# Two decode layers on one core: the feed-forward in one part of 448 columns, loads of 3.5 and 14 KB, and eight tiles of the last w2 in 512-column products

## The chip, the cores and the metric

The kernel runs on one core of a Trainium2 chip. The time is that of the whole kernel on the device, in microseconds; the median of 3 runs before the change is 705.18 us (705.13 to 705.38). Names of engines are those of the profile: PE is TensorE (PEld its weight loads), DVE VectorE, ACT ScalarE, POOL GpSimd, SP the SyncE whose queue issues nearly all loads.

## The reference

Four tokens (B = 4, one position each, D = 512) go twice through an attention block with a cache and a gated feed-forward; both layers use the same weights and the same cache. All is float32.

```python
def _A_ref(x, k_cache, v_cache, wq, wo):   # Hq 32, Hkv 8, Sk 4096, Dh 128
    q = (x @ wq).reshape(B, Sq, Hq, Dh).transpose(0, 2, 1, 3)
    k, v = jnp.repeat(k_cache, 4, axis=1), jnp.repeat(v_cache, 4, axis=1)
    p = _softmax(jnp.einsum("bhqd,bhkd->bhqk", q, k) * Dh ** -0.5)
    return jnp.einsum("bhqk,bhkd->bhqd", p, v).transpose(0, 2, 1, 3).reshape(B, Sq, Hq * Dh) @ wo
def _B_ref(x, w1, w3, w2):                 # F = 1792
    return (_silu(x @ w1) * (x @ w3)) @ w2
for layer in range(2):
    x = x + _A_ref(_layernorm(x), k_cache, v_cache, wq, wo)
    x = x + _B_ref(_layernorm(x), w1, w3, w2)
```

## The kernel before

Nearly all of the time is reading: keys, values and weights, for two layers, about 298 MB. One large SBUF tile, `arena` (218 pieces of 1 KB in each of the 128 partitions), receives every load. `plan` is the list of all loads in order; `pump` issues as many of them on the SP queue as find room, and `done` and `vacate` give room back (and call `pump`) when the products that read a load have been recorded. So a load is issued once the PE instruction that last read its place is through; the list order is fixed. Eight semaphores serve the loads in turn, so a load also waits for the landing of the eighth load before it. Around the first layer's feed-forward the places are given out by hand (`slots`, seven places of 4 KB in a row, and `RING`); elsewhere the first free stretch is taken.

The chain of a layer is: attention over 8 key/value groups, `project_o` (times wo, summed in `x_ps`), `collect` (residual and mean), then `feed_forward`, and after the first layer `collect` again and the next layer's queries. The order of the instructions on each engine is that of the code (manual schedule). `busy(n)` puts n products of 128 columns on PE whose result nobody reads (L292).

The 1792 columns of w1 and w3 are cut into four blocks of 448 (`FJ`), one for each 32-row group of PSUM; so a product of one 128-row chunk of x with all columns is four matmuls that write to `s_ps` (w1) or `o_ps` (w3). Before the change each block is again in two parts: the first 256 columns (`FA`) and the last 192 (`FB`). In `feed_forward` part a of w1 and w3 is done first (L561, L566), `gate` and `join` (L530, L535) make its h = silu(w1 x) (w3 x), then part b of w1 (L573), the transposes of h's first 256 columns (L577) and `tiles`, part b of w3, `join` of the last 192 columns (L593) and the transposes of those (`tail_tiles`, L595). In layer 0 (`keep`), `down` multiplies pairs of w2 tiles, its first call stands between the products of w3's part b (L591), and products with `busy` stand after most chunks. In layer 1 the output is made with swapped roles (`columns`, L550: the four 128-column blocks of a w2 tile go to four row groups of `x_ps`, so that the result comes out 128 columns wide). The 8 tiles of 16 rows in `few` (L555; w2's first tile cut up, loaded as `w2s` by `aside`) are multiplied in two halves, L588 and L608; the 13 other tiles follow in L610 to L614. At last `y` (L664) is copied from `x_ps` and stored.

The loads of layer 0 are 512 KB (a parts, w2) and 384 KB (b parts) each; in layer 1 w1 and w3 come in two loads each, 16 KB and 12 KB per partition, and tiles 1 to 13 of w2 in loads of 4, 4, 2, 2 and 1 tiles.

Of the kernel before, what the change touches and what calls it, by code (L numbers as in the profile page):

```python
# [9 lines left out]
AF = mybir.ActivationFunctionType  # L10
# [10 lines left out]
NI = BK // P  # L21
GW = SK * B
FJ = F // 4
FA = 2 * P
FB = FJ - FA
WT = 14
FEW = 16
EPS = 1e-5
SCALE = DH ** -0.5
# [9 lines left out]
def tile_decode_layers(ctx: ExitStack, tc: tile.TileContext, x, kt, v, wq, wo, w1, w3, w2, w2s, out):  # L39
# [48 lines left out]
    def load(src, per, keys, at=None):  # L88
        plan.append((src, per, keys, at))
# [9 lines left out]
    def weights(name, src, layer, parts, per, at=None, first=0):  # L99
        r = 0  # L100
        for n in parts:
            load(src[:, r * KB:(r + n) * KB], per, [(name, layer, first + r // per + j) for j in range(n // per)],
                 None if at is None else at + r)
            r += n

# [10 lines left out]

    def piece(name, i, at):

        w, layer, lo, n, per = {"w1a": (w1, 0, 4 * i, 4, 4), "w3a": (w3, 0, 4 * i, 4, 4),
                                "w1b": (w1, 0, 16 + 3 * i, 3, 3), "w3b": (w3, 0, 16 + 3 * i, 3, 3),  # L120
                                "w2": (w2, 0, 4 * i, 4, 2), "half": (kt[TURN], 1, 4 * i, 4, 4)}[name]
        weights(name, w[:, lo * KB:(lo + n) * KB], layer, (n,), per, at, 2 * i if name == "w2" else i)

    RING = KEPT + 64
    slots = [WO] + [RING + 4 * i for i in (5, 4, 3, 2, 1, 0)]
    for i in range(4):
        piece("w1a", i, (slots[6], slots[1], slots[2], slots[3])[i])
    for i in range(4):
        piece("w3a", i, (slots[4], slots[5], slots[0], slots[6])[i])
    for i in range(4):  # L130
        piece("w1b", i, RING + 21 - 3 * i)
    for i in range(2):
        piece("w3b", i, RING + 9 - 3 * i)
    piece("w2", 0, slots[0])
    for i in range(2, 4):
        piece("w3b", i, RING + 9 - 3 * i)
    for i in range(1, 7):
        piece("w2", i, slots[i])
# [25 lines left out]
    def pump():  # L164
        while state["next"] < len(plan):
            src, per, keys, at = plan[state["next"]]
            n = src.shape[-1] // KB
# [12 lines left out]
            if a is None:  # L180
                return
            nc.sync.dma_start(arena[:, a * KB:(a + n) * KB], src)  # L182
            i = state["next"]
            if i == 0:
                nc.sync.dma_start(xt[:8], x[:8])
            left[i] = (len(keys), a, n)
            for j, key in enumerate(keys):
                where[key] = (a + j * per, per, i)
            state["next"] += 1

    def loaded(*key):
        a, n, _ = where[key]
        return arena[:, a * KB:(a + n) * KB]
# [102 lines left out]
    def chunk(k):  # L296
        return p[:, k * P:(k + 1) * P]
# [219 lines left out]
    def feed_forward(layer, mean):  # L517
        keep = layer < LAYERS - 1
        h = p[:, 0:FJ]

        def product(name, ps, lo, n, fill=(0, 0, 0, 0), ks=range(KC)):
            for k in ks:
                w = loaded(name, layer, k)
                for j in range(4):
                    nc.tensor.matmul(ps[32 * j:32 * j + 32, lo:lo + n], x32[:, k, :], w[:, j * n:(j + 1) * n],  # L525
                                     start=(k == 0), stop=(k == KC - 1))
                done(name, layer, k)
                busy(fill[k] if keep else 0)

        def gate(lo, n):  # L530
            a = h[:, lo:lo + n]
            nc.scalar.activation(a, s_ps[:, lo:lo + n], AF.Sigmoid, scale=rstd)
            nc.vector.scalar_tensor_tensor(a, s_ps[:, lo:lo + n], rstd, a, op0=ALU.mult, op1=ALU.mult)

        def join(lo, n):  # L535
            a = h[:, lo:lo + n]
            nc.vector.scalar_tensor_tensor(a, o_ps[:, lo:lo + n], rstd, a, op0=ALU.mult, op1=ALU.mult)
# [12 lines left out]
        def columns(rows, m, w, last=False):  # L550
            for k in range(KC):
                nc.tensor.matmul(x_ps[32 * k:32 * k + B, 0:P], hT[rows, m, :], w[rows, k * P:(k + 1) * P],  # L552
                                 start=False, stop=last)
# [7 lines left out]
        product("w1a", s_ps, 0, FA, (0, 0, 2, 0))  # L561
# [4 lines left out]
        product("w3a", o_ps, 0, FA, (2, 2, 2, 2))  # L566
        if not keep:
            for k in range(KC):
                nc.tensor.matmul(x_ps[32 * k:32 * k + B, 0:P], xt[:, k, :], ident, start=True, stop=False)
            busy(4)  # L570
        gate(0, FA)
        join(0, FA)
        product("w1b", s_ps, FA, FB, (1, 1, 1, 1))  # L573
        if keep:
            gate(FA, FB)
            nc.scalar.activation(spare, half, AF.Exp)
        for i in range(2):  # L577
            nc.tensor.transpose(t_ps[:, i, :], h[:, i * P:(i + 1) * P], ident)
        if not keep:
            for u in range(8):  # L580
                nc.tensor.matmul(t_ps[0:FEW, 2, B * u:B * u + B], h[0:32, FEW * u:FEW * u + FEW], ident[0:32, 0:B],
                                 start=True, stop=True)
            busy()
        tiles(0, 8)
        if not keep:
            nc.vector.tensor_copy(hT[0:FEW, WT:WT + 8, :], t_ps[0:FEW, 2, 0:8 * B].rearrange("p (u b) -> p u b", b=B))
            gate(FA, FB)
            few(0, 4)  # L588
        product("w3b", o_ps, FA, FB, (1, 2, 1, 1), range(0, 2))
        if keep:  # L590
            down(0)  # L591
        product("w3b", o_ps, FA, FB, (1, 2, 1, 1), range(2, KC))
        join(FA, FB)  # L593

        def tail_tiles():  # L595
            nc.tensor.transpose(t_ps[:, 2, :], h[:, FA:FA + P], ident)
            for u in (0, 64):
                nc.tensor.matmul(t_ps[u:u + 64, 3, 0:64], h[u:u + 64, FA + P:FJ], ident[u:u + 64, u:u + 64],
                                 start=True, stop=True)
            tiles(8, 6)  # L600

        if keep:
            for i in range(1, WT // 2):
                if i == 4:
                    tail_tiles()
                down(i)
            return
        few(4, 8)  # L608
        tail_tiles()
        for m in range(1, WT):  # L610
# [96 lines left out]
```

## Time and profile before

| | |
|---|---|
| median of 3 runs | 705.18 us (705.13 to 705.38) |
| span of the profiled execution, first to last instruction | 705.4 us |
| its time around the span | not listed; the span alone is 0.2 us above the median |
| PE, PEld, DVE, ACT busy | 405.0, 136.0, 85.2, 38.0 us |
| DMA over the span | 298.85 MB, mean 424 GB/s |
| mean granted PE clock | 0.814 of full speed |

The profile is one execution. Its page gives busy times by engine, the span in 40 slices, the queues of the DMA engines, the chain of work that ended last, and groups of instructions. Views of the trace give the same for a stretch of time: the timeline (start, duration, engine, line, operation, tiles and shapes, count, and in brackets the engine's idle time before it and what ended it), the windows (busy time of each engine, granted clock and DMA share of each stretch), the waits, and the DMA queues. A matmul of float32 counts as two instructions in the profile, and one in the program's order below.

### The profile page before, as it was taken

The numbers are of one execution on the slowest core, as the hardware profiler recorded it, in microseconds if no ns is written. First come the engines' busy times: TensorE is split into PE (matmuls) and PEld (weight loads), VectorE is DVE, ScalarE is ACT, GpSimd is POOL, SyncE is SP. The second block draws the span as 40 slices with busy tenths as digits, with TensorE's granted clock in tenths as the row PEclk, the third lists the DMA queues.
The fourth block names the chain that finished last, engine by engine and source line by source line (L and its number), as shares of the span: only waits on it lengthen the run. The fifth ranks groups of instructions, "written<-read, shape, count | busy, mean of one in ns | idle before, by whom it ended". The sixth has DMA issues, their size and how long they took to land. (4 is left out here: it accounts for less than half of the span.)

```text
span 705.4 us, 7077 instructions
## 1 busy us (share of the span) xinstructions
PE 405.0 (57%) x3172; PEld 136.0 (19%) x3172; DVE 85.2 (12%) x291; ACT 38.0 (5%) x87; POOL 3.5 (0%) x11
## 2 busy tenths in 40 slices
PE   2555453555565453547788884365564545367686
PEld 1112111111111111112243321011111111112244
DVE  2001010101001010101111111020000101010120
ACT  0000000000000000002001000000000000000100
POOL 0000000000000000000000000000000000000000
PEclk9976687767778777779999997588787878787899
DMA  9999999999999999999999999999999999999996
GB/s 417 428 406 461 425 420 421 461 417 431 439 431 432 427 443 420 442 417 429 409 403 406 394 438 447 431 427 439 436 427 435 432 439 425 431 423 430 424 423 261
DMA packets 13605, 298.85 MB, mean 424 GB/s; under 512 B 1655, under 2 KB 1783, under 8 KB 6263
## 3 DMA queue, kind: packets, MB, share of 16 engines
q1 hardware_dynamic: 13440, 298.39, 99.0%
q8 instruction: 25, 0.41, 0.2%
q14 instruction: 5, 0.04, 0.0%
q10 hardware_dynamic: 135, 0.01, 0.0%
HBM read 298.33 MB, written 0.07 MB: 423 GB/s over the span
## 5 line engine op out<-in xcount | busy, mean ns | idle before, releaser
L457 PE MATMUL o_ps<-arena 128*32 128x512 f32 x1024 | 143.3, 707 | 148.1 <-DMA arena<-in_v 135.2
L410 PE MATMUL s_ps<-arena,qpad 128*32 128x512 f32 x1020 | 148.1, 734 | 90.3 <-DMA arena<-in_kt 90.3
L457 PEld LDWEIGHTS o_ps<-arena 128*32 128x32 f32 x1024 | 36.9, 127 | 251.9 <-issue 221.1
L410 PEld LDWEIGHTS s_ps<-arena,qpad 128*32 128x32 f32 x1020 | 39.3, 132 | 182.8 <-issue 175.9
L466 DVE SCALAR_TENSOR_TENSOR p<-o_ps,parts,p 128x512 f32<-128x512 f32 x16 | 12.0, 750 | 266.0 <-PE o_ps L457 266.0
L420 DVE TENSOR_REDUCE top<-s_ps 128x1 f32<-128x512 f32 x16 | 11.1, 691 | 195.3 <-PE s_ps L410 195.3
L292 PE MATMUL m_ps<-ident,rows 128*32 128x256 f32 (+1 forms) x96 | 24.1, 352 | 0.8 <-DVE xpad L335 0.8
L464 ACT ACTIVATE p<-o_ps,parts 128x512 f32<-128x512 f32 x16 | 11.0, 687 | 188.5 <-PE o_ps L457 182.3
L348 PE MATMUL o_ps<-arena,xpad 128*32 128x512 f32 x112 | 16.0, 698 | 7.5 <-DMA arena<-in_wq 7.5
L443 PE MATMUL t_ps<-ident,p 128*128 128x128 f32 x64 | 10.9, 295 | 13.5 <-ACT p L437 13.5
L470 PE MATMUL t_ps<-ident,p 128*128 128x128 f32 x64 | 10.5, 286 | 13.9 <-DVE p L466 13.8
L492 PE MATMUL x_ps<-arena,qT 128*4 128x512 f32 x112 | 13.8, 592 | 6.6 <-DVE qT L478 3.5
L430 ACT ACTIVATE f<-d 128x1 f32<-128x1 f32 x16 | 3.2, 203 | 249.8 <-DVE d L428 249.8
L437 ACT ACTIVATE p<-s_ps,top 128x512 f32<-128x512 f32 x16 | 10.9, 684 | 76.0 <-PE t_ps L470 76.0
L444 DVE COPY arena<-t_ps 128x512 f32<-128x512 f32 x16 | 11.1, 691 | 9.2 <-PE t_ps L443 9.2
L292 PEld LDWEIGHTS m_ps<-ident,rows 128*32 128x32 f32 x96 | 10.1, 110 | 10.7 <-issue 3.5
L470 PEld LDWEIGHTS t_ps<-ident,p 128*128 128x128 f32 x64 | 6.7, 140 | 28.0 <-DVE p L466 28.0
L443 PEld LDWEIGHTS t_ps<-ident,p 128*128 128x128 f32 x64 | 7.0, 145 | 22.3 <-ACT p L437 19.2
L525 PE MATMUL o_ps<-arena,xpad 128*32 128x192 f32 (+1 forms) x128 | 8.1, 360 | 1.5 <-DMA arena<-in_w 1.4
L525 PE MATMUL s_ps<-arena,xpad 128*32 128x192 f32 (+1 forms) x128 | 8.1, 358 | 1.4 <-DMA arena<-in_w 1.4
L485 PE MATMUL x_ps<-arena,qT 128*4 128x256 f32 x88 | 6.6, 379 | 2.3 <-DMA arena<-in_w 1.6
L552 PE MATMUL x_ps<-arena,qT 128*4 128x128 f32 (+1 forms) x168 | 5.9, 271 | 2.2 <-DMA arena<-in_w 2.1
(105 smaller groups left out, 139.4 us busy)
## 6 DMA issues: line engine op xcount, KB each, us to landing
arena<-in_v SPq DMA_DIRECT2D x4, 4096.0 KB, 39.7
arena<-in_w SPq DMA_DIRECT2D x17, 512.0 KB, 14.1
arena<-in_kt SPq DMA_DIRECT2D x8, 1024.0 KB, 9.9
arena<-in_kt SPq DMA_DIRECT2D x2, 4096.0 KB, 18.5
arena<-in_wq SPq DMA_DIRECT2D x1, 7168.0 KB, 40.1
arena<-in_v SPq DMA_DIRECT2D x3, 2048.0 KB, 32.3
arena<-in_wo SPq DMA_DIRECT2D x1, 4096.0 KB
arena<-in_kt SPq DMA_DIRECT2D x2, 2048.0 KB
```

The costliest lines, as they stand in the source:

```text
L292: nc.tensor.matmul(m_ps[0:32, (4 - w) * P:], rows, ident.unsqueeze(1).broadcast_to([P, w, P]), start=True, stop=True)
L348: nc.tensor.matmul(ps[32 * k:32 * k + 32, :], xpad[:, 32 * k + lo:32 * k + lo + 32], w[:, k, :], start=first, stop=last)
L410: nc.tensor.matmul(s_ps[32 * b:32 * b + 32, :], qpad[:, 32 * b + lo:32 * b + lo + 32], k[:, j, :], start=(blk == 0), stop=(blk == NB - 1))
L420: nc.vector.tensor_reduce(top[:, 0:1], s_ps, axis=AX.X, op=ALU.max, negate=True)
L443: nc.tensor.transpose(t_ps[:, i, :], p[:, i * P:(i + 1) * P], ident)
L444: nc.vector.tensor_copy(pT.rearrange("p i r -> p (i r)"), t_ps.rearrange("p i r -> p (i r)"))
L457: nc.tensor.matmul(o_ps[32 * b:32 * b + 32, :], pT[:, i, 32 * b:32 * b + 32], w[:, b, :], start=(i == 0), stop=(i == NI - 1))
L464: nc.scalar.activation(p, o_ps, AF.Copy, scale=st["parts"][:, 0:1])
L466: nc.vector.scalar_tensor_tensor(p, o_ps, st["parts"][:, 1:2], p, op0=ALU.mult, op1=ALU.add)
L470: nc.tensor.transpose(t_ps[:, j, :], p[:, j * P:(j + 1) * P], ident)
L492: nc.tensor.matmul(x_ps[r:r + B, :], left(2 * i + n), w(n), start=first, stop=False)
L525: nc.tensor.matmul(ps[32 * j:32 * j + 32, lo:lo + n], x32[:, k, :], w[:, j * n:(j + 1) * n], start=(k == 0), stop=(k == KC - 1))
```

## The change

`feed_forward` handles all 448 columns in one part. w1 and w3 are loaded as half chunks: 3.5 KB per partition in layer 0 (16 loads of 448 KB in place of 8 of 512 and 8 of 384), and 14 KB in layer 1 (four such loads in place of 16, 16, 12 and 12 KB). A half chunk has two of the four column blocks, so its product is two matmuls of 448 columns, in row groups 0 and 1 or 2 and 3 (`product`). `gate` and `join` run once, over 448 columns; `join`, the five transposes and the `tiles` copy come after the whole of w3. The `busy` calls inside the products are gone; `busy(4)` stands behind `join`. In layer 0 all w2 loads stand after all w3 loads, and all seven `down` calls after `tiles`. In layer 1 all of `few` comes after the transposes, tiles 1 to 8 of w2 are multiplied whole (`WIDE`: 4 output rows, 512 columns, four row groups of `o_ps`), `o_ps` is copied to `p`, and four products with `rows` add its row groups into `x_ps`; tiles 9 to 13 go through `columns` as before.

```diff
-FA = 2 * P
-FB = FJ - FA
+HALF = 2 * FJ / 256
+WIDE = 9
...
-    for i in range(4):
-        piece("w1a", i, (slots[6], slots[1], slots[2], slots[3])[i])
...
+    for n, (name, i) in enumerate([(name, i) for name in ("w1", "w3") for i in range(2 * KC)]):
+        piece(name, i, slots[(n + 6) % 7])
     for i in range(7):
-        piece("half", i + 1, slots[i])
+        piece("w2", i, slots[(i + 1) % 7])
+    for i in range(7):
+        piece("half", i + 1, slots[(i + 1) % 7])
...
-    for part, per, at in (("a", 4, 0), ("b", 3, 16)):
-        for name, w in (("w1", w1), ("w3", w3)):
+    for name, w in (("w1", w1), ("w3", w3)):
+        for i in range(2):
             aside()
-            weights(name + part, w[:, at * KB:(at + 4 * per) * KB], 1, (4 * per,), per)
+            weights(name, w[:, 14 * i * KB:14 * (i + 1) * KB], 1, (14,), HALF, None, 4 * i)
...
+        def product(name, ps):
+            for i in range(2 * KC):
+                w = loaded(name, layer, i)
+                for j in range(2):
+                    r = 32 * (2 * (i % 2) + j)
+                    nc.tensor.matmul(ps[r:r + 32, 0:FJ], x32[:, i // 2, :], w[:, j * FJ:(j + 1) * FJ],
+                                     start=(i < 2), stop=(i >= 2 * KC - 2))
+                done(name, layer, i)
...
+        def turned():
+            for i in range(3):
+                nc.tensor.transpose(t_ps[:, i, :], h[:, i * P:(i + 1) * P], ident)
+            for u in (0, 64):
+                nc.tensor.matmul(t_ps[u:u + 64, 3, 0:64], h[u:u + 64, 3 * P:FJ], ident[u:u + 64, u:u + 64],
+                                 start=True, stop=True)
...
+        gate()
...
+        product("w3", o_ps)
+        join()
+        busy(4)
+        turned()
         if keep:
+            tiles(0, WT)
+            for i in range(WT // 2):
                 down(i)
             return
+        for u in range(8):
+            nc.tensor.matmul(t_ps[0:FEW, 3, P - 8 * B + B * u:P - 8 * B + B * u + B], h[0:32, FEW * u:FEW * u + FEW], ident[0:32, 0:B],
+                             start=True, stop=True)
+        tiles(0, WT)
+        nc.vector.tensor_copy(hT[0:FEW, WT:WT + 8, :], t_ps[0:FEW, 3, P - 8 * B:P].rearrange("p (u b) -> p u b", b=B))
+        few(0, 8)
+        for m in range(1, WIDE):
+            r = 32 * (m % 4)
+            nc.tensor.matmul(o_ps[r:r + B, :], hT[:, m, :], loaded("w2", layer, m), start=(m < 5), stop=(m >= WIDE - 4))
+            done("w2", layer, m)
+        nc.vector.tensor_copy(p, o_ps)
+        for k in range(KC):
+            nc.tensor.matmul(x_ps[32 * k:32 * k + B, 0:P], rows[:, 0:B], chunk(k), start=False, stop=False)
+        for m in range(WIDE, WT):
             columns(slice(0, P), m, loaded("w2", layer, m), m == WT - 1)
             done("w2", layer, m)
-            if m in (4, 8):
+            if m == WIDE + 1:
                 busy(2)
```

The line numbers of the changed kernel are lower by 8 to 22 than those of the kernel before.

How the end of layer 1 stands on PE, before: from the second part of w1 to the last product. L525 is `product`, L578, L596 and L598 are transposes of h, L581 the turned 16-row tiles, L552 `columns` and `few`, L292 `busy`.

```order
L525 MATMUL s_ps<-arena,xpad 32x192 x16
L578 MATMUL t_ps<-ident,p 128x128 x2
L581 MATMUL t_ps<-ident,p 16x4 x8
L292 MATMUL m_ps<-ident,rows 32x128
L552 MATMUL x_ps<-arena,qT 4x128 x16
L525 MATMUL o_ps<-arena,xpad 32x192 x16
L552 MATMUL x_ps<-arena,qT 4x128 x16
L596 MATMUL t_ps<-ident,p 128x128
L598 MATMUL t_ps<-ident,p 64x64 x2
L552 MATMUL x_ps<-arena,qT 4x128 x16
L292 MATMUL m_ps<-ident,rows 32x256
L552 MATMUL x_ps<-arena,qT 4x128 x16
```

And the same place now, to the last product; L517 is `product`, L551, L553 and L577 the transposes, L541 `few` and `columns`, L584 the whole tiles, L588 the sum over row groups, L283 `busy`.

```order
L517 MATMUL o_ps<-arena,xpad 32x448 x16
L283 MATMUL m_ps<-ident,rows 32x256 x2
L551 MATMUL t_ps<-ident,p 128x128 x3
L553 MATMUL t_ps<-ident,p 64x64 x2
L577 MATMUL t_ps<-ident,p 16x4 x8
L541 MATMUL x_ps<-arena,qT 4x128 x32
L584 MATMUL o_ps<-arena,qT 4x512 x8
L588 MATMUL x_ps<-p,rows 4x128 x4
L541 MATMUL x_ps<-arena,qT 4x128 x8
L283 MATMUL m_ps<-ident,rows 32x256
L541 MATMUL x_ps<-arena,qT 4x128 x12
```

Work that stood between the products of w1 and w3 (transposes, 16 products of `few`) and beside the last join (16 more) now stands behind the last join; nothing stands on PE between the two loads of w3. One copy of 512 columns on DVE, between L584 and L588, is new.

On the SP queue, the loads of the first layer's feed-forward before the change (from the second load of w3's part b on; each row with the semaphores that it waits for, DMAHW being those of earlier loads):

```order
L182 DMA arena_66<-in_w3 128x768 [waits DMAHW1_49,PE_49]
L182 DMA arena_66<-in_w2 128x1024 [waits DMAHW2_49,PE_49]
L182 DMA arena_66<-in_w3 128x768 [waits DMAHW3_49,PE_49]
L182 DMA arena_66<-in_w3 128x768 [waits DMAHW4_49]
L182 DMA arena_66<-in_w2 128x1024 [waits DMAHW5_49,PE_49]
```

and its first loads now:

```order
L173 DMA arena_66<-in_w1 128x896 [waits DMAHW4_49]
L173 DMA arena_66<-in_w1 128x896 [waits DMAHW5_49,DMAHW7_49,DVE_49,PE_49]
L173 DMA arena_66<-in_w1 128x896 [waits DMAHW6_49]
L173 DMA arena_66<-in_w1 128x896
L173 DMA arena_66<-in_w1 128x896 [waits DMAHW0_49]
```

The first w2 load no longer stands among those of w3; the second w1 load now goes to the first place of wo (`slots[0]`), which a w3 load took before, and waits on DVE for the copies of `stash` (L496).

More of the change, by code (lines that the diff above doesn't have):

```diff
@@ L101, in weights @@
         for n in parts:
-            load(src[:, r * KB:(r + n) * KB], per, [(name, layer, first + r // per + j) for j in range(n // per)],
+            load(src[:, int(r * KB):int((r + n) * KB)], per, [(name, layer, first + int(r / per) + j) for j in range(int(n / per))],
                  None if at is None else at + r)
@@ L117, in piece @@
     def piece(name, i, at):
-        w, layer, lo, n, per = {"w1a": (w1, 0, 4 * i, 4, 4), "w3a": (w3, 0, 4 * i, 4, 4),
-                                "w1b": (w1, 0, 16 + 3 * i, 3, 3), "w3b": (w3, 0, 16 + 3 * i, 3, 3),
+        w, layer, lo, n, per = {"w1": (w1, 0, HALF * i, HALF, HALF), "w3": (w3, 0, HALF * i, HALF, HALF),
                                 "w2": (w2, 0, 4 * i, 4, 2), "half": (kt[TURN], 1, 4 * i, 4, 4)}[name]
-        weights(name, w[:, lo * KB:(lo + n) * KB], layer, (n,), per, at, 2 * i if name == "w2" else i)
+        weights(name, w[:, int(lo * KB):int((lo + n) * KB)], layer, (n,), per, at, 2 * i if name == "w2" else i)
     RING = KEPT + 64
     slots = [WO] + [RING + 4 * i for i in (5, 4, 3, 2, 1, 0)]
-    for i in range(4):
-        piece("w1a", i, (slots[6], slots[1], slots[2], slots[3])[i])
[L128 to L138, printed above, removed]
+    for n, (name, i) in enumerate([(name, i) for name in ("w1", "w3") for i in range(2 * KC)]):
+        piece(name, i, slots[(n + 6) % 7])
     for i in range(7):
-        piece("half", i + 1, slots[i])
+        piece("w2", i, slots[(i + 1) % 7])
+    for i in range(7):
+        piece("half", i + 1, slots[(i + 1) % 7])
     ring["to"] = len(plan) - 1
@@ L166, in pump @@
             src, per, keys, at = plan[state["next"]]
-            n = src.shape[-1] // KB
+            w = src.shape[-1]
+            n = -(-w // KB)
             if isinstance(per, slice):
@@ L181, in pump @@
                 return
-            nc.sync.dma_start(arena[:, a * KB:(a + n) * KB], src)
+            nc.sync.dma_start(arena[:, a * KB:a * KB + w], src)
             i = state["next"]
@@ L192, in loaded @@
         a, n, _ = where[key]
-        return arena[:, a * KB:(a + n) * KB]
+        return arena[:, int(a * KB):int((a + n) * KB)]
     def done(*key):
@@ L519, in feed_forward, with gate, join @@
         h = p[:, 0:FJ]
[L521 to L537, printed above, removed]
+        def product(name, ps):
[6 more added lines that the diff above has]
+                done(name, layer, i)
+        def gate():
+            nc.scalar.activation(h, s_ps[:, 0:FJ], AF.Sigmoid, scale=rstd)
+            nc.vector.scalar_tensor_tensor(h, s_ps[:, 0:FJ], rstd, h, op0=ALU.mult, op1=ALU.mult)
+        def join():
+            nc.vector.scalar_tensor_tensor(h, o_ps[:, 0:FJ], rstd, h, op0=ALU.mult, op1=ALU.mult)
         def tiles(lo, n):
@@ L558, in few @@
                 columns(slice(0, FEW), WT + u, arena[:, at:at + 2 * KB])
+        def turned():
[4 more added lines that the diff above has]
+                                 start=True, stop=True)
         sq = squares()
-        product("w1a", s_ps, 0, FA, (0, 0, 2, 0))
+        product("w1", s_ps)
         rstd = deviation(sq, total(flat(sq)))
@@ L565, in feed_forward @@
             nc.vector.tensor_tensor(xt, xc, mu.unsqueeze(1).broadcast_to([P, KC, B]), op=ALU.add)
-        product("w3a", o_ps, 0, FA, (2, 2, 2, 2))
-        if not keep:
             for k in range(KC):
                 nc.tensor.matmul(x_ps[32 * k:32 * k + B, 0:P], xt[:, k, :], ident, start=True, stop=False)
[L570 to L573, printed above, removed]
+        gate()
         if keep:
-            gate(FA, FB)
             nc.scalar.activation(spare, half, AF.Exp)
-        for i in range(2):
-            nc.tensor.transpose(t_ps[:, i, :], h[:, i * P:(i + 1) * P], ident)
@@ L579, in feed_forward @@
[L579 to L589, printed above, removed]
@@ L590, in feed_forward @@
-        if keep:
[L591 to L605, printed above, removed]
+        product("w3", o_ps)
@@ L606, in feed_forward @@
+        join()
+        busy(4)
+        turned()
+        if keep:
+            tiles(0, WT)
+            for i in range(WT // 2):
                 down(i)
             return
-        few(4, 8)
-        tail_tiles()
-        for m in range(1, WT):
+        for u in range(8):
[3 more added lines that the diff above has]
+        nc.vector.tensor_copy(hT[0:FEW, WT:WT + 8, :], t_ps[0:FEW, 3, P - 8 * B:P].rearrange("p (u b) -> p u b", b=B))
@@ L679 @@
     w1, w3, w2 = np.asarray(B_w1), np.asarray(B_w3), np.asarray(B_w2)
-    w13 = [np.concatenate([a.reshape(KC, P, 4, FJ)[..., s].transpose(1, 0, 2, 3).reshape(P, -1)
-                           for s in (slice(0, FA), slice(FA, FJ))], axis=1) for a in (w1, w3)]
+    w13 = [a.reshape(KC, P, F).transpose(1, 0, 2) for a in (w1, w3)]
     w2j = w2.reshape(4, FJ, D)
@@ L692 @@
         "wo": lay(wo.reshape(HKV, REP, DH, D).transpose(2, 0, 1, 3)).reshape(P, HKV * REP * D),
-        "w1": lay(w13[0]),
-        "w3": lay(w13[1]),
+        "w1": lay(w13[0]).reshape(P, KC * F),
+        "w3": lay(w13[1]).reshape(P, KC * F),
         "w2": lay(np.concatenate([full, rest], axis=1)).reshape(P, WT * D),
```

## The prediction

> **What bounds the kernel now.** I read the page's slices first, then the end of the chain of waits, then the timeline of the last feed-forward.
>
> ```profile
> DMA  9999999999999999999999999999999999999996
> q8 instruction: 25, 0.41, 0.2%
> 645.28 39.28 DMA arena<-in_w
> ...
> 684.62 16.68 DMA arena<-in_w
> ...
> 701.35 0.62 PE x_ps L552 x16
> ...
> 702.00 0.45 PE x_ps L552 x8
> ...
> 702.47 0.29 DVE p L665
> ```
>
> The DMA engines are full in 39 slices of 40, so until the last weights only bytes and gaps in loading count. The chain (start, length, what) ends in a w2 load that lands near 701.97; eight PE instructions (tile 13) take 0.45, and the copy of the output starts at 702.47. What moves that copy moves the time.
>
> ```profile
> 688.66 1.51 PE L525 MATMUL s_ps<-arena,xpad 128*32 128x192 f32 x32 [0.56 <-DMA arena<-in_w]
> 692.89 1.51 PE L525 MATMUL o_ps<-arena,xpad 128*32 128x192 f32 x32 [0.45 <-DMA arena<-in_w]
> 694.33 1.05 PE L552 MATMUL x_ps<-arena,qT 16*4 16x128 f32 x32
> 694.46 0.42 DVE L537 SCALAR_TENSOR_TENSOR p<-o_ps,rstd,p 128x192 f32<-128x192 f32 x1 [2.81 <-PE o_ps L525]
> 695.31 0.33 PE L596 MATMUL t_ps<-ident,p 128*128 128x128 f32 x1
> ...
> 695.57 0.33 PE L598 MATMUL t_ps<-ident,p 64*64 64x64 f32 x4
> 695.83 1.06 PE L552 MATMUL x_ps<-arena,qT 128*4 128x128 f32 x32
> 696.70 0.59 PE L292 MATMUL m_ps<-ident,rows 128*32 128x256 f32 x2
> 698.82 1.06 PE L552 MATMUL x_ps<-arena,qT 128*4 128x128 f32 x32 [1.52 <-DMA arena<-in_w]
> ```
>
> The last of w3 is there at 692.85. PE is through with it, half of the 16-row tiles (694.33), the transposes, w2 tiles 1 to 4 (695.83) and a filler by 697.3, and then waits 1.52 us for tiles 5 to 8. So PE has some 1.5 us of room here, and the end is set by loading.
>
> **The change, part by part.** *Loads.* Bytes are the same; only row sizes differ.
>
> ```profile
> 368.00:372.00 4.00, 3.35 (x43) 1.71 (x42) 0.51 (x2) 1.91 (x3) 0.00 (x0) 1.00 1.03 402
> 376.00:380.00 4.00, 3.35 (x35) 1.17 (x27) 0.12 (x1) 0.00 (x0) 0.00 (x0) 1.00 1.02 408
> arena<-in_w SPq DMA_DIRECT2D x8, 384.0 KB, 7.5
> arena<-in_kt SPq DMA_DIRECT2D x7, 512.0 KB, 8.3
> 345.17 1.29 DVE L496 COPY kept<-arena 128x512 f32<-128x512 f32 x2 [5.42 <-DMA arena<-in_wo]
> 355.18 0.11 PEld L485 LDWEIGHTS x_ps<-arena,qT 128*4 128x4 f32 x8 [0.66 <-DMA arena<-in_wo]
> ```
>
> The windows (the last number is GB/s) have 402 where 3 KB rows dominate and 408 at 4 KB rows. 7.34 MB of w1 and w3 take 18.26 us at one rate and 17.99 at the other; 3.5 KB lies between, as the mixture did: 0, within 0.15 us either way. The 14 KB rows lie between 12 and 16 KB: 0 likewise. *Layer 0's order.* A load is under way 7.5 to 8.3 us from issue to landing, all of it queueing, and that covers what is moved. The second w1 load, with all loads behind it on SP, now waits for the stash copies, which end at 346.46, while wo is still landing until 355.18. The last join, the transposes and the first `down` now follow all of w3, about 3 us after its landing, so SP issues the next key loads up to 1 us later. A half chunk on PE (448 columns, 0.95 us by the sum below) stays under the 1.14 us in which 448 KB arrive at 402 GB/s, so PE keeps up. I take 0; without the cover each of these would cost its delay, 1 to 3 us, once.
>
> *The last feed-forward.* Here the work moves behind the last w3 load, and I add it up from 692.89 on at full clock. Durations come from the rows above and these:
>
> ```profile
> 345.12 3.62 PE L492 MATMUL x_ps<-arena,qT 128*4 128x512 f32 x32 [2.77 <-DMA arena<-in_wo]
> 664.08 0.69 DVE L444 COPY arena<-t_ps 128x512 f32<-128x512 f32 x1 [1.11 <-PE t_ps L443]
> 677.60 0.66 PE L470 MATMUL t_ps<-ident,p 128*128 128x128 f32 x4 [0.53 <-DVE p L466]
> 678.18 0.14 PEld L292 LDWEIGHTS m_ps<-ident,rows 128*32 128x32 f32 x2 [0.17 <-issue]
> 686.86 0.40 PE L569 MATMUL x_ps<-ident,xt 128*4 128x128 f32 x8
> 687.11 0.48 DVE L537 SCALAR_TENSOR_TENSOR p<-o_ps,rstd,p 128x256 f32<-128x256 f32 x1 [0.47 <-PE o_ps L525]
> 690.47 0.55 PE L581 MATMUL t_ps<-ident,p 32*16 32x4 f32 x16
> 691.39 1.05 PE L552 MATMUL x_ps<-arena,qT 16*4 16x128 f32 x32
> ```
>
> A PE group's length holds about 0.2 us of pipeline behind its last matmul; 16 matmuls of 512 columns take 3.42 without it, so four side by side cost 1.67 ns a column.
>
> - w3's last load: 8 matmuls of 448 columns, 2 x 448 x 1.67 ns = 1.50, plus 0.2: to 694.59. (16 of 192 columns took 1.51.)
> - `join` over 448 columns: 192 took 0.42 and 256 took 0.48, so 0.67, with 0.06 of hand-over on each side: to 695.38. `busy(4)` runs beside it.
> - Transposes: four take 0.58 until the next group, so three 0.44; the two of 64 columns 0.26 (L598 to L552); the turned 16-row tiles 0.55: to 696.63.
> - Two DVE copies: 690.47 + 0.55 to 691.39 is 0.37: to 697.00.
> - All 32 products of `few`: twice 0.86 (695.83 to 696.70 is one such group): to 698.72.
> - Tiles 1 to 8 whole: 8 x 512 x 1.67 / 4 = 1.71, plus 0.2: to 700.63. Their loads are there by 698.82, so PE no longer waits.
> - The new copy, 512 columns: 0.69 and twice 0.06: to 701.44. Behind it on DVE stands only the output's copy, but on PE the four products that wait for it hold up tiles 9 to 13.
> - Four products of 128 columns 0.21; tiles 9 and 10 0.43; `busy(2)` 0.4; tiles 11 and 12 0.43; tile 13 0.21 + 0.2: to 703.32.
>
> Before, that point was 702.00 + 0.45 = 702.45. So PE's chain replaces the load as what is late, by **+0.9 us**; the removed wait of 1.52 is more than eaten by the join, by the 16 products of `few` that had stood ahead of it (0.86), by the copy with its four products (1.0) and by the wider product. Errors of the steps: 0.3 either way, and 0.4 for when w3 lands.
>
> *The clock.* The fillers and the work between w3's two loads go. How PE's clock answers:
>
> ```profile
> 645.34 3.64 PE L457 MATMUL o_ps<-arena 128*32 128x512 f32 x32
> 647.68:651.10 3.42, 1.30 (x15) 0.16 (x4) 0.00 (x0) 0.69 (x1) 0.00 (x0) 1.00 1.02 441
> 651.10:654.51 3.41, 0.00 (x0) 0.00 (x0) 0.00 (x0) 0.00 (x0) 0.00 (x0) 0.50 1.03 442
> 654.51:657.92 3.41, 2.61 (x16) 0.77 (x20) 0.00 (x0) 0.00 (x0) 0.00 (x0) 0.50 0.96 413
> 655.31 4.91 PE L457 MATMUL o_ps<-arena 128*32 128x512 f32 x32 [6.33 <-DMA arena<-in_v]
> 671.58:674.99 3.41, 1.78 (x14) 0.71 (x13) 0.00 (x0) 0.00 (x0) 0.00 (x0) 1.00 0.99 413
> 688.64:692.05 3.41, 3.36 (x78) 2.53 (x82) 0.60 (x3) 0.42 (x1) 0.00 (x0) 1.00 0.99 412
> ```
>
> The rows give PE's busy time first and the granted clock as third number from the end. The clock changes on a grid of 3.41 us. A stretch with 1.30 us of work is followed by half clock, though PE stopped (645.34 + 3.64 = 648.98) only 2.1 us before; 1.78 us keeps it whole. At half clock the same 32 instructions took 4.91 instead of 3.64. Now 688.64 to 692.05 holds 3.36 us of work. After the change w3's first load lands near 688.0 (42 KB per partition lie ahead of its end instead of 44, against 688.66), its 8 products end at 689.75, and PE is idle for 3.1 us until 692.89. A stretch of the grid that begins between 688.4 and 690.8 has at most 1.35 us of work, and 2.4 of 3.41 is 70% of the places that the grid can have, since nothing ties it to the program. Then half clock falls on the chain above: a stretch from 692.05 to 695.47 would do 1.29 us of the 1.50 in 2.58, which is 1.3 late; later stretches catch transposes and `few` and lose up to 1.6. Bounds: 0 and 1.7 (half a stretch); I take **+1.4**, since the 1.30 row is the nearest. The sum is 0.9 + 1.4 = +2.3; the span of 705.4 stands 0.2 above the median, so I put the difference on the median: 707.5.
>
> On the clock the Trainium skill (TensorE: Matmul & The Clock Gate, HAM oscillation) speaks for the other outcome: its rule is that PE idle gaps must not exceed about 3.4 us. By it 3.1 us would be harmless and the sum 706.1; the trace differs, with a fall 2.1 us after the last matmul.
>
> **The rivals.**
>
> *The clock holds.* The grid falls well, or a gap under a full stretch doesn't count. For it: 30% of the grid's places. The chain still grows by 0.9: 706.1 (705.6 to 706.5), within 0.2%, which is 1.4 us and about what can be told from no change.
>
> *Loading still sets the end, and ends sooner: the other side.* The DMA engines do not finish together:
>
> ```profile
> 698.00:700.00 2.00, 1.18 (x34) 0.97 (x34) 0.00 (x0) 0.00 (x0) 0.00 (x0) 1.00 0.53 207
> 700.00:702.00 2.00, 1.35 (x35) 0.68 (x33) 0.00 (x0) 0.00 (x0) 0.00 (x0) 1.00 0.11 33
> q8 instruction: 2, 0.03, 2.1%
> ```
>
> The last row is the queue view from 695 to 702.4: two instruction packets took 2.1% of 16 engines' 7.4 us, 1.24 us each. If one sat on the engine that trails at the end, the change, with 97 fewer matmuls in program order, could take it from there: landing 1.24 sooner, 703.9. It decides only if PE's chain after w3 is under 8 us where I count 10.4. Against it is every row above. The Trainium skill (Runtime: NRT & Kernel Launch, Instruction fetch mechanics) has blocks of 16 KiB; 0.41 MB in 25 packets agrees.
>
> *Layer 0 starves.* If its loads are issued too late, the DMA share of 1.02 to 1.03 there falls and 1 to 3 us come on top: 708 to 710. Against it are the 7.5 us of queue.
>
> **How the numbers follow.** Clock falls and chain grows: 0.62, at 706.9 to 708.2, all of it slower by over 0.2% (above 706.6). Clock holds: 0.27, of it 0.25 within 0.2%. Loading still sets the end: 0.07, of it 0.03 faster and 0.04 within. Layer 0 starves: 0.04, of it 0.03 slower and 0.01 within. Faster 0.03; same 0.25 + 0.04 + 0.01 = 0.30; slower 0.62 + 0.02 + 0.03 = 0.67. The range takes in the first two cases with the errors of the steps: 705.7 to 708.2.
>
> **What would show it.** In the changed kernel the chain of waits should end in PE and DVE from w3's last landing on, with the copy of 512 columns in it, and no PE wait on a w2 load from tile 5 on. PE should be idle about 3 us before w3's last load, and the windows should show a clock of 0.50 for 3.41 us from between 691.8 and 694.2. The DMA share between 350 and 385 should stay at 1.02. I am wrong if the last w2 load still ends the chain, if the clock is 1.00 there, or if w3's last landing moves by more than 0.5 us.

## The result, and the profile after

The changed kernel takes 710.93 us (median of four: 708.54, 708.85, 713.01, 713.71) against 705.28 us before: 1.0079 times as long, with an interval of 1.0062 to 1.0096. The forecast was 707.5 us, with a range up to 708.2: the direction was right and the size too small. The four values also lie in two pairs 4.6 us apart; those of the kernel before lie within 0.6 us.

The profile is of the 708.85 us execution (span 706.9). The end of its chain of waits (start, length, what):

```profile
674.46 17.11 DMA arena<-in_w
...
691.62 1.71 PE o_ps L517 x16
693.33 0.84 PE m_ps L283 x4
694.17 0.51 PE t_ps L551 x3
694.68 0.26 PE t_ps L553 x4
694.94 0.49 PE t_ps L577 x16
...
695.82 1.93 PE x_ps L541 x64
697.74 3.55 PE o_ps L584 x16
...
701.32 0.70 DVE p L586
...
702.07 0.40 PE x_ps L588 x8
702.47 0.44 PE x_ps L541 x16
...
704.06 0.29 DVE p L644
```

The chain no longer ends in a w2 load. From the last w3 load on (691.57) it is PE and DVE to the output's copy at 704.06. One length is odd: the eight 512-column tiles (L584) take 3.55 us, where 1.9 was forecast. The windows, cut along the clock's grid, say why (busy time of PE, PEld, DVE, ACT, POOL with instruction counts; granted clock, DMA share, GB/s):

```profile
687.43:690.84 3.41, 1.60 (x16) 0.30 (x14) 0.57 (x1) 0.00 (x0) 0.00 (x0) 1.00 0.97 408
690.84:694.26 3.42, 2.65 (x21) 0.98 (x22) 0.68 (x1) 0.00 (x0) 0.00 (x0) 1.00 1.00 417
694.26:697.67 3.41, 3.02 (x87) 2.37 (x87) 0.30 (x2) 0.00 (x0) 0.00 (x0) 1.00 0.89 357
697.67:701.08 3.41, 3.41 (x20) 0.41 (x16) 0.00 (x0) 0.00 (x0) 0.00 (x0) 0.50 0.19 73
```

There is one half-clock stretch, as forecast, but not where it was forecast. The stretch with the gap between w3's two loads has 1.60 us of work and is followed by full clock. The stretch after which the clock falls, 694.26 to 697.67, has PE busy for 3.02 us of 3.41. What is special in it is the kind of work: from 695.82 to 697.67 these are products that fill 16 of the array's 128 rows (`few`).

### The profile page after: what moved, and what is told of

It is laid out like the page before. It is cut to its first block, busy times and chain, and to the rows that moved or that the text cites. A ratio compares the mean times of both kernels' runs of the same rounds, so it can differ in the third digit from the quotient of the medians.

```text
span 706.9 us, 6683 instructions
## 1 busy us (share of the span) xinstructions
PE 407.9 (58%) x2978; PEld 130.4 (18%) x2978; DVE 84.9 (12%) x286; ACT 37.5 (5%) x85; POOL 3.5 (0%) x11
## 5 line engine op out<-in xcount | busy, mean ns | idle before, releaser
L448 PE MATMUL o_ps<-arena 128*32 128x512 f32 x1024 | 147.1, 724 | 146.8 <-DMA arena<-in_v 133.4
L461 PE MATMUL t_ps<-ident,p 128*128 128x128 f32 x64 | 10.5, 286 | 13.9 <-DVE p L457 13.8
L283 PE MATMUL m_ps<-ident,rows 128*32 128x256 f32 (+1 forms) x70 | 17.7, 363 | 0.8 <-DVE xpad L326 0.8
L517 PE MATMUL o_ps<-arena,xpad 128*32 128x448 f32 x64 | 10.5, 548 | 3.9 <-DMA arena<-in_w 3.8
L517 PE MATMUL s_ps<-arena,xpad 128*32 128x448 f32 x64 | 9.8, 545 | 0.7 <-DMA arena<-in_w 0.5
L283 PEld LDWEIGHTS m_ps<-ident,rows 128*32 128x32 f32 x70 | 7.2, 110 | 9.9 <-issue 4.0
L339 PEld LDWEIGHTS o_ps<-arena,xpad 128*32 128x32 f32 x112 | 3.6, 121 | 17.2 <-DMA arena<-in_wq 8.9
```

The costliest lines, as they stand in the source:

```text
L283: nc.tensor.matmul(m_ps[0:32, (4 - w) * P:], rows, ident.unsqueeze(1).broadcast_to([P, w, P]), start=True, stop=True)
L339: nc.tensor.matmul(ps[32 * k:32 * k + 32, :], xpad[:, 32 * k + lo:32 * k + lo + 32], w[:, k, :], start=first, stop=last)
L448: nc.tensor.matmul(o_ps[32 * b:32 * b + 32, :], pT[:, i, 32 * b:32 * b + 32], w[:, b, :], start=(i == 0), stop=(i == NI - 1))
L461: nc.tensor.transpose(t_ps[:, j, :], p[:, j * P:(j + 1) * P], ident)
L517: nc.tensor.matmul(ps[r:r + 32, 0:FJ], x32[:, i // 2, :], w[:, j * FJ:(j + 1) * FJ], start=(i < 2), stop=(i >= 2 * KC - 2))
```

## The experiments

**Which layer.** Two kernels, each with the changed feed-forward in one layer and that of before in the other.

```diff
-        feed_forward(layer, collect())
+        (feed_forward_apart if layer == 0 else feed_forward)(layer, collect())
```

That is the one with the change in layer 1 alone (`feed_forward_apart` is the function of before, with its loads); the other has `layer == 1`.

> Layer 1's feed-forward is the changed one; layer 0's, with its loads of 4 KB and 3 KB and its order, is that of before. Theory T (what was predicted: the time is lost behind the last w3 load): all of the loss is here, the lower runs near 708.7 us and, if the two values of the changed kernel (708.7 and 713.4) come from where the half clock falls in that tail, both values appear. Rival L (layer 0 loads more slowly or starves): 706 to 707 us and one value.

> Layer 0's feed-forward is the changed one, with its loads of 3.5 KB; layer 1's is that of before. Theory T: 705.1 to 705.7 us, one value, DMA share 1.02 between 346 and 385. Rival L: it holds the part of the loss that the chain behind w3 does not explain, 707 to 708 us in the lower runs, and the upper runs near 712 if the two values come from here.

With the change in layer 1 alone: 706.71, 708.26, 708.38, 708.56, 708.83, 711.00, 712.91 and 712.92 us, median 708.70, 1.0058 of before (1.0037 to 1.0079). In layer 0 alone: 705.10 us, 0.9994 (0.9985 to 1.0002). So nothing is lost in layer 0, all of the loss and all of the spread is in the last feed-forward, and the two pairs were four draws out of a spread of 7 us. The profiled execution of the first kernel is one of the long ones (712.91 us), and its windows show what these do differently:

```profile
688.86:692.27 3.41, 0.31 (x4) 0.16 (x8) 0.00 (x0) 0.00 (x0) 0.00 (x0) 1.00 0.98 402
692.27:695.69 3.42, 3.42 (x19) 1.12 (x12) 0.68 (x1) 0.00 (x0) 0.00 (x0) 0.50 0.99 405
695.69:699.10 3.41, 3.02 (x74) 2.18 (x76) 0.30 (x2) 0.00 (x0) 0.00 (x0) 1.00 0.62 247
699.10:702.51 3.41, 3.41 (x36) 0.94 (x32) 0.00 (x0) 0.00 (x0) 0.00 (x0) 0.50 0.03 8
702.51:705.93 3.42, 2.61 (x36) 0.98 (x32) 0.69 (x1) 0.00 (x0) 0.00 (x0) 0.50 0.00 0
705.93:709.34 3.41, 2.23 (x30) 0.83 (x22) 0.29 (x1) 0.00 (x0) 0.00 (x0) 0.50 0.00 0
```

Here the grid lies 2 us earlier against the program. The gap between w3's loads fills a stretch (0.31 us of work), so the next one, with w3's last product, runs at half clock: the forecast mechanism. Then the stretch with the 16-row products (3.02 us busy again) is followed by half clock to the very end. In this kernel's chain the steps are:

```profile
691.96 2.96 PE o_ps L529 x16
694.93 1.28 PE m_ps L295 x4
...
697.82 2.42 PE x_ps L553 x64
700.24 3.57 PE o_ps L596 x16
...
708.24 0.29 DVE p L755
```

w3's last product takes 2.96 us for 1.71, the tiles 3.57, and the output's copy starts 16.3 us after w3's landing (691.92), against 12.5 in the other profile.

**Fillers, and the wide products.** The first kernel adds fillers in layer 1 around the suspected places, the second takes the 512-column products with their copy away.

```diff
                 done(name, layer, i)
+                if name == "w3" and not keep and i == KC - 1:
+                    busy(10)
...
                 columns(slice(0, FEW), WT + u, arena[:, at:at + 2 * KB])
+                busy(u % 2)
...
+        busy(2)
         tiles(0, WT)
```

```diff
-WIDE = 9
+WIDE = 1
...
-        for m in range(1, WIDE):
...
-        nc.vector.tensor_copy(p, o_ps)
-        for k in range(KC):
-            nc.tensor.matmul(x_ps[32 * k:32 * k + B, 0:P], rows[:, 0:B], chunk(k), start=False, stop=False)
...
```

> The changed kernel with fillers in layer 1 alone: ten between w3's two loads, two ahead of the tile copies, one behind every other 16-row product. They cost about 1.3 us of PE's chain at full clock. Theory T: the clock stays 1.00 from 690 to 703, the half-clock stretch (1.66 us) is gone, and the lower value is 708.2 to 708.6 us; if the upper value is the clock too it is gone, and all runs agree. Rival L: the two values stay 4.6 us apart, both about 1 us higher.

> The changed kernel with tiles 1 to 8 in 128-column products straight into x_ps, so without the 512-column copy and the four products that add it up. Theory T: the chain behind w3 is shorter by the copy (0.70) and the hand-overs and four products (0.4), so 1.0 to 1.2 us less in each value: near 707.6 and 712.3 us. Rival W (the wait on the copy was hidden, or loads set the end): no difference, 708.7 and 713.4 us.

The fillers made it 710.92 us (five runs, 710.22 to 711.12; 1.0072, 1.0059 to 1.0085), 2.5 us above what was expected. The long values are gone, but a half-clock stretch is still there, behind a stretch in which PE was busy all the time:

```profile
689.41:692.83 3.42, 3.42 (x30) 1.49 (x26) 0.42 (x1) 0.00 (x0) 0.00 (x0) 1.00 0.99 414
692.83:696.24 3.41, 3.41 (x44) 1.68 (x37) 0.75 (x2) 0.00 (x0) 0.00 (x0) 1.00 0.99 405
696.24:699.65 3.41, 3.41 (x72) 1.65 (x70) 0.23 (x2) 0.00 (x0) 0.00 (x0) 1.00 0.62 242
699.65:703.07 3.42, 3.42 (x26) 0.99 (x18) 0.00 (x0) 0.00 (x0) 0.00 (x0) 0.50 0.01 2
```

That refutes the prediction's rule, which went by PE's busy time: 3.41 us of 3.41 was not enough. The timeline has the small products there in pieces of 16 with a filler behind each:

```profile
698.37 0.61 PE L543 MATMUL x_ps<-arena,qT 16*4 16x128 f32 x16
698.92 0.41 PE L283 MATMUL m_ps<-ident,rows 128*32 128x128 f32 x2
```

From start to start a piece fills 0.55 us. Three of them and 0.40 us of the fourth lie in that stretch, 2.05 us; the rest, 1.4 us, is below the 1.60 that held the clock above. That made the 16-row products the suspect; it did not show it.

Without the wide products: 709.17 us (706.95 to 711.60; 1.0053, 1.0034 to 1.0071). The spread hides a difference of 1 us, but its profile has the half clock at the same place in the grid as the changed kernel's, so those two can be compared: w3 lands at 692.03 and the output's copy starts at 703.28, 11.25 us later, against 12.49. The copy and the four products cost 1.24 us; 1.0 to 1.2 was expected.

**The kernel before, and each cause alone.** The first of four kernels is the kernel before, unchanged. The others are the changed kernel with the fillers in the gap alone; with 128 rows for 16 in the small products (which leaves tile 0's share out of the output); and with tile 0 whole.

```diff
                 done(name, layer, i)
+                if name == "w3" and not keep and i == KC - 1:
+                    busy(10)
```

```diff
-                at = (where["few"] + 2 * u) * KB
-                columns(slice(0, FEW), WT + u, arena[:, at:at + 2 * KB])
+                for k in range(KC):
+                    nc.tensor.matmul(x_ps[32 * k:32 * k + B, 0:P], hT[:, 1 + u, :], ident, start=False, stop=False)
```

```diff
-            aside()
...
-    weights("w2", w2[:, 2 * KB:], 1, (8, 8, 4, 4, 2), 2, None, 1)
+    weights("w2", w2, 1, (10, 8, 4, 4, 2), 2)
...
-        few(0, 8)
-        for m in range(1, WIDE):
+        for m in range(WIDE):
...
```

> The kernel before, unchanged, for its span beside its own time. Theory S (the profiled execution of before, span 705.4, was some 2 us longer than those that were timed): time minus span is 1.6 to 2.0 us as in the other kernels, so the span is 703.3 to 703.8; w3's last load lands near 691.6 and the last of w2 near 699.7, 1.3 and 2.2 us ahead of the profile of before. Rival: the span is 705.2 to 705.6 again, and the time is as long as the span in this kernel alone.

> The changed kernel with ten fillers (2.1 us) between w3's two loads in layer 1, and nothing else. Theory G (the upper value of 711 to 713 comes from the gap between w3's loads, when a stretch of the clock's grid falls in it): the upper value is gone, all runs lie within 708.0 to 709.5 us, and the one half-clock stretch that is left is that behind the 16-row products. Rival: runs above 711 us are still there.

> The changed kernel with the 32 products of 16 rows replaced by as many of 128 rows and the same 4 and 128 columns (the turned h tiles by the identity), so tile 0's share of the output is wrong. PE's busy time is the same. Theory R (the clock's monitor counts the rows at work, so a stretch of 16-row products passes for an idle one): no half clock from 697 to 701 in the lower runs, which come to 707.0 us; the upper runs keep only what the gap between w3's loads costs, 708.5 to 710. Rival C (any product with 4 columns passes for idle, or the stretch before it decides): half clock at the same place, 708.7 and 713 as in the changed kernel.

> The changed kernel with tile 0 of the last w2 loaded and multiplied whole (128 rows of 2 KB instead of 16 rows of 16 KB, the same bytes), as a ninth 512-column tile; the 8 turns, the second copy and the 32 products of 16 rows are gone. Theory T: PE's chain is 2.4 us shorter and without the half clock behind the small products, so the last w2 load sets the end again: 705.0 to 705.6 us in most runs, at most 706.5 where the gap's half clock falls on w3's product. Rival (the wide products and their copy are what costs): 707 us or more.

The kernel before ran at 705.29 us (0.9997, 0.9987 to 1.0007), and its profiled execution took 705.71 us with a span of 703.8. Its last lines on PE, and its chain:

```profile
691.69 1.51 PE L525 MATMUL o_ps<-arena,xpad 128*32 128x192 f32 x32
...
697.27 1.06 PE L552 MATMUL x_ps<-arena,qT 128*4 128x128 f32 x32 [1.17 <-DMA arena<-in_w]
```

```profile
684.22 15.54 DMA arena<-in_w
...
700.91 0.29 DVE p L665
```

So theory S holds: time minus span is 1.9 us here, and 1.6 to 2.2 in every run that lists both. By that the first profile of before, with a span of 705.4, was of an execution of 707.0 us or more, longer than any of the 75 timed runs of that kernel (704.99 to 706.98). In the usual execution the load that ends the wait of the last products lands 1.5 us sooner (699.76 for 701.30) and the output's copy starts 1.56 sooner (700.91 for 702.47), while w3 lands 1.3 us sooner (691.53 for 692.85; it is issued at 674.43 and takes 17.1 us).

With the gap filled: 707.26, 707.71, 708.46, 709.44, 710.38 and 712.03 us (ratio 1.0055, 1.0037 to 1.0073). I had expected 708.0 to 709.5 and nothing above 711; four of the six lie outside the first, and one above the second. If the 16-row products are all that is left, they alone can cost 4.6 us over the chain at full clock (707.4, below). That was not seen in a trace: the profiled execution of this kernel, 707.71 us, has the clock at 1.00 from 687 us to its end. With 128 rows: 707.01, 707.10, 708.16, 708.39, 710.09 and 710.72 us (1.0042, 1.0026 to 1.0057), none at the 713 of the changed kernel; by the times, the gap alone costs up to 3.3 us. Its profile fell on a place of the grid without any half clock, so it says nothing on rows, and six runs are few; the direct test is the next one. With tile 0 whole: 706.69 us (705.48 to 707.60; 1.0013, 1.0005 to 1.0022). That is 4 us better than the changed kernel, but 1.1 above what I expected (seven of the eleven runs lie above the 706.5 that was to be the most), and the profile has the half clock of the gap on w3's product, 2.97 us long:

```profile
688.23:691.65 3.42, 0.84 (x12) 0.16 (x8) 0.00 (x0) 0.00 (x0) 0.00 (x0) 1.00 1.00 422
691.65:695.06 3.41, 3.41 (x19) 1.11 (x12) 0.68 (x1) 0.00 (x0) 0.00 (x0) 0.50 0.99 408
```

**The rows by themselves, and both causes away.** Two kernels repeat the small products eight times, with 16 rows and with 128; the last two fill the gap in the kernel with 128 rows, and in that with tile 0 whole (the same `busy(10)`).

```diff
-        few(0, 8)
+        for _ in range(8):
+            few(0, 8)
```

> The changed kernel with the 32 products of 16 rows (4 and 128 columns) done eight times over, so some 14 us of them in one piece, longer than any place that the clock's grid can have (tile 0's share is added eight times). Theory R (a stretch of 16-row products passes for an idle one, though PE is busy all the time): the clock falls to 0.50 inside the piece, at the end of the first whole stretch of the grid in it at the latest (6.8 us), and stays there until its end, so the piece takes 19 to 25 us and the kernel 725 to 735 us. Rival: the clock stays 1.00, the piece takes 13.9 us, the kernel 719 to 722 us.

> The same with 128 rows (turned h tiles by the identity), as many products of the same 4 and 128 columns, so tile 0's share is wrong. Theory R: the clock stays 1.00 inside the piece, which takes 13.9 us; 719 to 722 us. Rival C (products of 4 columns pass for idle, whatever their rows): it falls as in the other kernel, 725 to 735 us.

> The changed kernel with both causes taken away: ten fillers between w3's two loads, and the 32 products with 128 rows for 16 (tile 0's share is wrong). PE's chain behind w3 is as long as before in instructions. Theory (gap and 16-row products are the only two causes of the half clock): no half clock behind 680 in any execution, so all runs lie together, 706.7 to 707.5 us, what the chain costs at full clock. Rival (a third cause): runs above 708.5 us remain.

> The kernel with tile 0 whole, and ten fillers between w3's two loads: the whole computation, without either cause. Theory: its runs lose the 1.2 us that w3's product lost at half clock, and lie together at 705.0 to 705.6 us, as before the change, with PE's chain and the last w2 load ending within 0.5 us of each other. Rival (the 706.7 of the kernel with tile 0 whole comes from something else): 706.7 us again.

The chains of the two long kernels show their 512 PE instructions of that line in one row each, 16 rows first:

```profile
695.87 24.85 PE x_ps L541 x512
```

```profile
698.14 14.16 PE x_ps L547 x512
```

and these are windows of the first, then of the second:

```profile
695.27:698.68 3.41, 3.02 (x113) 2.74 (x113) 0.30 (x2) 0.00 (x0) 0.00 (x0) 1.00 0.74 293
698.68:702.09 3.41, 3.41 (x72) 2.63 (x67) 0.00 (x0) 0.00 (x0) 0.00 (x0) 0.50 0.05 17
...
715.75:719.16 3.41, 3.41 (x72) 2.61 (x64) 0.00 (x0) 0.00 (x0) 0.00 (x0) 0.50 0.00 0
```

```profile
699.20:702.61 3.41, 3.41 (x132) 3.34 (x128) 0.00 (x0) 0.00 (x0) 0.00 (x0) 1.00 0.04 13
...
706.02:709.44 3.42, 3.42 (x136) 3.35 (x128) 0.00 (x0) 0.00 (x0) 0.00 (x0) 1.00 0.02 5
```

PE is busy without a break in both pieces. With 16 rows the clock falls 2.8 us into the piece and stays at 0.50 until its end; with 128 rows it stays at 1.00. The times, 733.48 and 721.58 us (one run each), both lie in the ranges that theory R gave; the second holds a half clock on w3's product too (3.21 us), ahead of the piece. So 16-row products let the clock fall as idleness does. The second kernel also multiplies the identity where the first multiplies w2, which was not tried apart. But products of 128 rows with loaded wo ran at 1.00 in the changed kernel (16 products with 4 output rows and 512 columns, 3.62 us from 344.97), so loaded data alone does not bring the clock down.

With both causes away eleven runs lie between 706.86 and 708.03 us (median 707.34; 1.0024, 1.0015 to 1.0033), where the same chain with the causes in it gave 706.71 to 713.71. The expectation reached only to 707.5, but nothing is above 708.5. Its windows are at 1.00 to the end, and its chain from w3's landing at 691.85 has:

```profile
691.89 1.71 PE o_ps L517 x16
...
697.93 1.77 PE o_ps L586 x13
...
702.46 0.29 DVE p L646
```

Tile 0 whole with the gap filled: 706.07 us (705.50 to 706.50), 1.0003 of before (0.9994 to 1.0012). That is 0.5 us more than I expected, but no measurable loss against the kernel before, and no gain either. Its end does not hang on the last load: the chain goes from the load of tiles 5 to 8, which lands at 697.64, through the wide products, the copy and the products behind it to the output's copy 3.9 us later.

```profile
665.15 32.49 DMA arena<-in_w
697.69 1.09 PE o_ps L580 x8
698.80 0.70 DVE p L582
...
701.53 0.29 DVE p L640
```

## Why the prediction was wrong, step by step

**What bounds the kernel before** was right, loading. But the numbers were of one execution that ended late, and the step "the span of 705.4 stands 0.2 above the median, so I put the difference on the median" failed: a span is some 1.9 us short of its own time, so that span belonged to a time near 707.3 us, not 705.18. For the sum this matters by 0.25 us: in the usual execution the end that the new chain has to beat is 1.56 us earlier, and the start of that chain 1.3 us earlier.

**Loads and layer 0**, costed at nothing: right. Layer 0's change alone gave 0.9994. w3's last load lands at 691.57 in the changed kernel and at 691.53 in the usual execution of before, and the last packets of w2 end near 699.2 and 699.8. The DMA share between 350 and 385 is 1.01; the forecast was 1.02.

**PE's chain**: its length was right. The forecast was 10.5 us from w3's landing to the output's copy at full clock; with both causes away it was 10.61 (691.85 to 702.46). Its price was mis-sized: +0.9 was forecast, and with both causes away the kernel is 0.24% slower than before, 1.7 us. In the profiles the output's copy starts 1.55 us later (702.46 for 700.91). Of the 0.65 us that the forecast lacks, 0.25 come from the late execution, 0.1 from the chain's length, and 0.3 from w3, which landed that much later in this one profile than in the usual execution of before.

**The clock** is the step that failed most. The gap behaved as forecast: with an empty stretch (0.31 us) half clock fell on w3's product, which took 1.25 us longer (1.3 was forecast), and with 1.60 us of work the clock held. With only this cause (128 rows, the gap left) the runs had a mean of 708.6 us, 1.2 above the 707.4 of the kernel with neither; +1.4 was forecast. But the prediction let only PE's idle time start a half-clock stretch, gave `few` and the tiles behind it full clock unless the gap had taken it, and set the bound at half a stretch, 1.7. That is the step that was wrong: the clock does not go by PE's busy time, and the term for the 16-row products, put at nothing, is 1.8 us. These products, gathered by this change into one piece of 1.93 us, start a half-clock stretch of their own, which can last into a second and third stretch. With only this cause (the gap filled) the mean was 709.2, 1.8 above. The two means are of six runs each, with standard errors of 0.6 and 0.7 us. The pieces add up to 705.3 + 1.7 + 1.2 + 1.8 = 710.0; twelve runs with this tail (the four of the changed kernel and eight with the change in layer 1 alone) have a mean of 710.1. That the two agree to 0.1 us is in part luck, by these errors.

The profile of before held a warning that the prediction did not use. At the end of its layer 0 PE is busy nearly all the time, and yet the clock falls at 384.8:

```profile
380.00:384.00 4.00, 3.52 (x36) 1.73 (x37) 0.65 (x4) 0.47 (x2) 0.00 (x0) 1.00 1.02 406
384.00:388.00 4.00, 3.74 (x22) 1.79 (x25) 0.96 (x5) 0.18 (x1) 0.00 (x0) 0.61 1.00 399
```

The last products ahead of the fall are those of L331 and L334 (383.27 to 384.62), which move only 4 and 16 columns. The same place falls in three later profiles, after stretches with 2.75 to 2.78 us of busy time in 3.41, and not in the others. That such products count for little too is a reading of this one place; no run tried it.

In the kernel before the same 32 products stand in two pieces of 1.05 us with full products on both sides, in stretches that are full of other work, and in its two profiles no half clock follows there.

**The spread** comes from the two causes: with both away, eleven runs lie within 1.2 us. That the grid's place decides how much they cost is how I read the two profiles: in that of 708.85 us the stretches begin at 687.43, in that of 712.91 at 685.45, while w3's last loads land within 0.4 us of each other and the tails are the same. That the grid's place explains every single run was not shown, since the runs without a profile do not tell their place. The Trainium skill (TensorE: Matmul & The Clock Gate, What's actually happening) calls the window of 3413 ns free-running, and these profiles agree: all changes lie on one grid of 3.41 us whose place against the program moved from run to run.

**The rivals.** "The clock holds" was forecast at 706.1; one execution of twelve with this tail, 706.71 us, is as short as those with neither cause. The Trainium skill (TensorE: Matmul & The Clock Gate, HAM oscillation) has the rule that speaks for this rival, no PE idle gaps over some 3.4 us. These runs do not bear it out: shorter gaps were followed by half clock, 2.58 us in the kernel with tile 0 whole (up to 691.34) and 3.21 us in the kernel with the change in layer 1 alone (timeline, the bracket is the wait):

```profile
691.96 2.96 PE L529 MATMUL o_ps<-arena,xpad 128*32 128x448 f32 x16 [3.21 <-DMA arena<-in_w]
```

"Loading still sets the end" and "layer 0 starves" did not happen.

## What to carry to other kernels

PE's busy time is not what holds its clock: products that use few rows of the array count for little. So gather them only where the clock may fall, keep them in short pieces among much full-row work (as the kernel before does; one filler behind every eight of them was not enough), or load such a tile with all its rows (here that took back 4.2 us of 5.6, by the clock and by a shorter chain together). Before a difference of spans is put on a median, check that the profiled execution is a usual one: its own time, not its span, must agree with the median. A chain that ends the kernel on PE and lets the clock fall can make its time a matter of where the grid falls, so one execution can be off by several microseconds.

## What the runs showed that was not expected

- A piece of 16-row products, PE busy without a break, lets the clock fall from 1.00 to 0.50 and keeps it there: 512 instructions took 24.85 us, and 14.16 with 128 rows and the same columns. Where between 16 and 128 rows this ends was not tried. The Trainium skill (TensorE: Matmul & The Clock Gate, What's actually happening) lets the clock follow how busy PE has been; these rows agree only if busy means how much of the array is at work, not time.
- At half clock a stretch with 2.61 us of busy time (702.51 to 705.93 above) was followed by half clock again, and one with the same 2.61 us in the profile of before (654.51 to 657.92, in the prediction) by full clock. At half clock products take about twice as long, so 2.61 us is the work of some 1.3 us at full clock (an estimate), as much as in the row of 1.30 after which the clock fell. So these rows do not show that it takes more work to come back than to stay.
- Nor is the 1.60 us that held the clock above a bound for PE's busy time: in the kernel with the change in layer 1 alone the stretch from 422.60 to 426.01 has 1.60 us as well, part of it transposes and sums of 16 columns, and half clock follows.
- The kernel before, whose end is set by loading, stayed within 2 us in 75 timed runs; the same arithmetic behind the same bytes spread over 7 us once a PE chain with the two causes in it set the end.
